# The first two batches of an attention and mixture-of-experts chain rescheduled: a pinned TensorE order, other slots, wider products, low bits on ScalarE

## The chip, the cores and the metric

One core of one Trainium2 chip. The metric is the time of one launch on the device in microseconds (us); each engine (TensorE or PE, VectorE or DVE, ScalarE or ACT, GpSimd or POOL, and SyncE or SP, which issues the transfers) has a queue of its own that it works off in order. A launch is timed three times, and once more with the hardware profiler.

## The reference

Three layers follow each other: Nystrom attention over 8 batches of 576 tokens and 8 heads, a gated feed-forward layer, and a soft mixture of 8 experts. Cut to what matters:

```python
# attention, per batch and head: m = 32 landmarks, the mean over 18 tokens each
A, Bm, C = sm(q, k_lm), sm(q_lm, k_lm), sm(q_lm, k)     # softmax(scale * a @ b.T)
Z = Bm.T / (norms of Bm)
for _ in range(6): Z = 2 * Z - Z @ Bm @ Z
x = A @ Z @ C @ v                                       # [4608, 512] over all batches
# gated feed-forward, d_ff = 1536
g = x @ w_gate; x = (g * sigmoid(g) * (x @ w_val)) @ w_out
# soft mixture of experts, 32 slots
logits = x @ phi
d = softmax over the 4608 tokens; c = softmax over the 32 slots
out = c @ experts(d.T @ x)          # each expert relu(s @ w1) @ w2
```

## The kernel before, in words

The kernel takes the eight batches one after another. x is never written out: for a batch the softmax A (kept as a high part EH and a low part EL of fp32, in the fp32r format) is multiplied by G = (Z C v) w, so that `g_product` (L739) forms for each of 12 chunks of 128 columns of d_ff (`j`) the product of the batch's small block `WB` with the weights `w` into PSUM tiles named g, and evicts them as a high part GH (ScalarE, L765) and a low part GL (VectorE, L779, called `g_low`). `mm3` (L939) then makes the gate (`pg`) and the value (`pv`) of one chunk and one half of 288 tokens with six matmuls each: 24 matmuls a chunk. `unit` (L948) evicts: ScalarE writes u = silu(pg) (L312), VectorE multiplies by pv into hT (L974). Where a pair (chunk, half) stands in `TANH`, silu is made with Tanh on ScalarE (L959) and one more VectorE instruction (L960), since Tanh lies in the same table as Exp, and the table need not be changed.

Around this main stream everything else is interleaved by hand. A chunk has four slots, 0 to 3, one after each group of six matmuls; slot n of a batch is 4 j + i, so a batch has 48. In a slot stand:

- `g_unit(b, j + 1)`, `logits` (eight matmuls of hT with `P_sb`, L794) and `transposes` (VectorE, L799), at the slot numbers of `u` (batches 1 to 7) and `u0` (batch 0);
- the steps of three generators, at the slots listed in `SCHED`: `attention` of the next batch (`at1` to `at3`, 34 steps: landmark sums L333, score products m_a and m_c L541, transposes m_t L631, m_v L653, six Newton products m_n L672, m_w L534), `a_softmax` of the next batch (`am1` to `am3`: maxima, Exp, sums, E), and `softmoe` of the batch before (`sm`, `sm1`: Exp of the logits, the transpose DN L867, the exchange of DN's quarters between partitions by twelve small transfers L879 or, for batch 6, by matmuls m_dr L882, then 144 small matmuls m_d L913 and their sums Sacc L923);
- in batch 0 alone: `conversion` of the float64 weights, twelve of w and twelve of w_out. ScalarE makes the top 32 bits (L176), VectorE shifts (L192) and ORs (L193); with `lw` set for a weight, one ScalarE instruction makes the low bits in place of VectorE's shifts. From w_out, `p_transposes` (m_wt L269), `p_product` (m_p L278) and `p_sum` (m_ps L284) make `P_sb`. The raw weights stream in through a few staging buffers, in the order `loads`; a buffer's next load is issued after its conversion.

Ahead of batch 0 stands its own attention (`first_attention`, until 39 us); behind batch 7 stand the experts and the output. PSUM has three buffers of the tag `x`, which g, m_a, m_c, m_t, m_n, m_v, m_d and the three of batch 0 share. The framework orders each engine's instructions by a planner of its own; `keep_order(PE, middle, ...)` (L1136) ties TensorE's to the order of the program from the mark `middle` on, which is set at batch 1 (L1099).

Of the kernel before, what the change touches and what calls it, by code (L numbers as in the profile page):

```python
# [22 lines left out]
NJ = DFF // 128  # L23
# [31 lines left out]
def nystrom_softmoe_kernel(  # L55
# [681 lines left out]
    def paired(b, j):  # L737
        return 0 < b < nb - 1 and not (b == nb - 2 and j >= NJ - 2)
# [209 lines left out]
    def unit(b, j, slot):  # L948
# [3 lines left out]
        for half in range(2):  # L952
            pg = psp.tile([128, 512], F32, tag="pg", name="pg", bufs=2)
            mm3(pg, b, j, 0, half)
            u = mp.tile([128, HALF], F32, tag="u", name="u", bufs=2)
            by_tanh = 0 < b < nb - 1 and (j, half) in TANH[b > 1]
            if by_tanh:

                act.activation(u, pg[:, 0:HALF], AF.Tanh, scale=0.5)  # L959
                dve.scalar_tensor_tensor(out=u, in0=u, scalar=1.0, in1=pg[:, 0:HALF], op0=ALU.add, op1=ALU.mult)  # L960
            else:
                in_order("silu", u, pg[:, 0:HALF], AF.Silu)
            slot(2 * half)
            pv = psp.tile([128, 512], F32, tag="pv", name="pv", bufs=2)
            mm3(pv, b, j, 1, half)
            o = hT[:, HALF * half:HALF * half + HALF]
            if b == 0 and S_["hp"][2 * j + half]:
                vt = spare[1][:, 128:416]
                act.copy(vt, pv[:, 0:HALF])
                pool.tensor_tensor(out=o, in0=u, in1=vt, op=ALU.mult)  # L970
            elif by_tanh:
                dve.scalar_tensor_tensor(out=o, in0=u, scalar=0.5, in1=pv[:, 0:HALF], op0=ALU.mult, op1=ALU.mult)
            else:
                dve.tensor_tensor(out=o, in0=u, in1=pv[:, 0:HALF], op=ALU.mult)  # L974
            slot(2 * half + 1)
# [5 lines left out]
    TANH = [{(5, 0), (5, 1), (6, 0)}, {(1, 1), (2, 0), (2, 1)}]  # L981
# [105 lines left out]
    for a in range(1, nb):  # L1087
        att, asm = attention(a), a_softmax(a)
        for gen, nm in ((att, "at"), (asm, "am")):
            for r in S_[nm + str(min(a, 3))]:  # L1090
                todo[48 * (a - 1) + r].append(gen)
        sm = softmoe(a - 1)
        for r in S_["sm1" if a == 1 else "sm"]:
            todo[48 * a + r].append(sm)
    prev = None
    n_ins = lambda: len(nc.cur_bb.bb.instructions)
    for b in range(nb):
        if b == 1:
            middle = n_ins()  # L1099
        for j in range(NJ):  # L1100
            p = prev
            def slot(i):
# [27 lines left out]
                if n == (46 if b == 0 else 45) and b + 1 < nb:  # L1130
                    g_unit(b + 1, 0)
                if n == (47 if b == 0 else 46):
# [212 lines left out]
```

## Time and profile before

| | us |
|---|---|
| three timed runs | 676.28, 674.23, 675.02 (median 675.02) |
| profiled execution, its own time | 674.4 |
| its span (first to last instruction) | 672.6 |
| TensorE busy in the span | 623.9 (93%) |
| VectorE busy | 478.0 (71%) |
| ScalarE busy | 298.8 (44%) |
| start to the first product of batch 0 (L748) | 39.2 |
| batch 0 (39.2 to 126.2) | 87.0 |
| batch 1 (126.2 to 201.0) | 74.8 |
| batches 2, 3, 4, 5, each | 65.9 |
| batch 6 | 63.9 |
| batch 7 (528.5 to 589.0) | 60.5 |

A batch ends where VectorE has written its last hT. A time of busy TensorE is from a matmul's start to its modelled end; matmuls overlap, so the distance from start to start tells more than the busy share. The mean granted clock of TensorE over the span is 0.984.

### The profile page before, as it was taken

What the parts mean: (1) busy time and instruction counts of PE and PEld (TensorE: products, weight loads), DVE (VectorE), ACT (ScalarE), POOL (GpSimd) and SP (SyncE); (2) the same over time, 40 slices, a digit from 0 to 9 for tenths busy, and PEclk for the clock granted to TensorE, in tenths of its full rate; (3) what the DMA queues carried; (4) which work ended last, traced back from release to release, by engine and by line L of the source; (5) the groups of instructions that cost most, each with busy time, mean ns of one, the idle gap of its engine ahead of it and who ended that gap; (6) DMA issues with size and microseconds to landing.
All of it is one profiled execution on the core that took longest, in us unless ns stands there. A gap on an engine that the chain in (4) does not pass through costs nothing. (4 is left out here: it accounts for less than half of the span.)

```text
span 672.6 us, 18315 instructions
## 1 busy us (share of the span) xinstructions
PE 623.9 (93%) x7591; PEld 465.8 (69%) x7591; DVE 478.0 (71%) x1154; ACT 298.8 (44%) x764; POOL 73.3 (11%) x81
## 2 busy tenths in 40 slices
PE   5699999998999999999999999999999999989991
PEld 2575667784877877787787778777778777843560
DVE  4999989878578777868785978597856645550441
ACT  2566875445438323732383338233823442320441
POOL 0400012013011101110111012001300000010000
PEclk9799999998999999999999999999999999999996
DMA  8788773233222222222222222122120595699999
GB/s 281 271 322 331 269 280 129 87 113 116 73 72 83 75 72 73 84 75 73 72 86 73 71 87 76 69 71 72 57 86 2 160 378 184 220 288 348 348 369 337
DMA packets 63299, 106.47 MB, mean 158 GB/s; under 512 B 4977, under 2 KB 33009, under 8 KB 61681
## 3 DMA queue, kind: packets, MB, share of 16 engines
q1 hardware_dynamic: 63216, 105.32, 47.1%
q8 instruction: 59, 0.97, 0.6%
q14 instruction: 24, 0.19, 0.1%
HBM read 91.24 MB, written 12.58 MB: 154 GB/s over the span
## 5 line engine op out<-in xcount | busy, mean ns | idle before, releaser
L312 ACT ACTIVATE u<-pg 128x288 f32<-128x288 f32 x174 | 71.9, 413 | 138.4 <-PE pg L945 130.8
L974 DVE TENSOR_TENSOR hT<-u,pv 128x288 f32<-128x288 f32 x174 | 77.7, 447 | 40.1 <-PE pv L945 36.3
L945 PE MATMUL pg<-EH,GH 128*128 128x288 f32 x384 | 93.9, 324 | 2.6 <-ACT GH L765 1.6
L779 DVE TENSOR_TENSOR GL<-g,GH 128x512 fp32r<-128x512 f32 (+1 forms) x122 | 66.4, 572 | 37.7 <-ACT GH L765 37.6
L945 PE MATMUL pg<-EH,GL 128*128 128x288 f32 x384 | 85.7, 299 | 1.7 <-DVE GL L779 1.5
L945 PE MATMUL pv<-EH,GH 128*128 128x288 f32 x384 | 84.0, 298 | 0.0
L945 PE MATMUL pg<-EL,GH 128*128 128x288 f32 x384 | 83.5, 296 | 0.0
L945 PE MATMUL pv<-EL,GH 128*128 128x288 f32 x384 | 82.6, 296 | 0.0
L945 PE MATMUL pv<-EH,GL 128*128 128x288 f32 x384 | 82.2, 295 | 0.0
L765 ACT CAST GH<-g 128x512 fp32r<-128x512 f32 (+1 forms) x122 | 54.2, 495 | 55.0 <-PE g L748 54.9
L945 PEld LDWEIGHTS pg<-EH,GH 128*128 128x128 f32 x384 | 60.0, 189 | 22.8 <-issue 15.5
L799 DVE STREAM_TRANSPOSE HB<-hT 128x576 f32<-128x576 f32 x96 | 74.3, 774 | 1.8
L945 PEld LDWEIGHTS pg<-EH,GL 128*128 128x128 f32 x384 | 62.2, 188 | 4.7 <-DVE GL L779 3.8
L945 PEld LDWEIGHTS pv<-EH,GH 128*128 128x128 f32 x384 | 61.6, 188 | 2.6 <-issue 1.2
L945 PEld LDWEIGHTS pg<-EL,GH 128*128 128x128 f32 x384 | 61.8, 188 | 0.9 <-issue 0.9
L945 PEld LDWEIGHTS pv<-EL,GH 128*128 128x128 f32 x384 | 61.5, 188 | 0.9 <-issue 0.9
L945 PEld LDWEIGHTS pv<-EH,GL 128*128 128x128 f32 x384 | 61.6, 188 | 0.5 <-issue 0.5
L748 PE MATMUL g<-w,WB 64*32 64x512 f32 (+1 forms) x976 | 56.4, 510 | 0.4 <-ACT WB L535 0.4
L794 PE MATMUL l<-hT,P_sb 128*32 128x160 f32 (+1 forms) x768 | 45.2, 298 | 0.8 <-DVE hT L974 0.6
L794 PEld LDWEIGHTS l<-hT,P_sb 128*32 128x32 f32 x768 | 15.2, 108 | 39.8 <-DVE hT L974 16.5
L913 PE MATMUL m_d<-HB,HB 32*32 32x384 f32 x864 | 38.4, 514 | 2.6 <-DMA HB<-DN 2.3
L913 PE MATMUL m_d<-HB,DN 32*32 32x384 f32 x288 | 37.7, 514 | 0.0
(248 smaller groups left out, 946.4 us busy)
## 6 DMA issues: line engine op xcount, KB each, us to landing
k<-in_kT_dram SPq DMA_DIRECT2D x52, 288.0 KB, 3.7
ffn<-in_w_dram SPq DMA_DIRECT2D x13, 1024.0 KB, 9.0
ffn<-in_w_dram SPq DMA_DIRECT2D x24, 512.0 KB, 9.0
HB<-in_w_cat_dram SPq DMA_DIRECT2D x8, 1024.0 KB, 8.0
v<-in_v_dram SPq DMA_DIRECT2D x8, 1024.0 KB, 5.8
q<-in_qT_dram SPq DMA_DIRECT2D x28, 288.0 KB, 3.0
HB<-in_w_out_dram SPq DMA_DIRECT2D x12, 512.0 KB, 5.8
wr<-in_w_cat_dram SPq DMA_DIRECT2D x4, 1024.0 KB, 8.7
```

Source lines behind the costliest of these rows:

```text
L312: i = act.activation(*a, **kw)
L748: pe.matmul(gs[r][32 * hp:32 * hp + 32, 0:256 * n].rearrange("p (u f) -> p u f", u=n), WB[b % 2][64 * r:64 * r + 64, hp, :], w[64 * r:64 * ...
L765: act.copy(H_, g)
L779: dve.tensor_tensor(out=GL, in0=g, in1=GH, op=ALU.subtract)
L794: pe.matmul(L[32 * c:32 * c + 32, 0:32 * k], P_sb[:, j, :], main[:, 0:k, c, :], start=j == 0, stop=j == NJ - 1)
L799: dve.transpose(HB[b % 2][:, S * j:S * j + S].rearrange("p (t r) -> p t r", r=32), hT[:, 0:S].rearrange("p (t r) -> p t r", r=32))
L913: pe.matmul(ms[a][32 * g:32 * g + 32, 0:384].rearrange("p (j f) -> p j f", j=NJ), d_of(a, g, k), hb[32 * a:32 * a + 32, :, 4 * k + g, :], ...
L945: pe.matmul(ps[:, 0:HALF], G_t[b, j, q, sel_][h], e[:, q, ts_], start=n == 0, stop=n == 5)
L974: dve.tensor_tensor(out=o, in0=u, in1=pv[:, 0:HALF], op=ALU.mult)
```

## The change

Nine things, all of them in the order and the place of work; what is computed stays the same.

1. `middle` is set ahead of batch 0, so TensorE's order is the program's there too.
2. `u0` becomes (1, 1, 1): in batch 0 too, `g_unit`, `logits` and `transposes` stand in slot 1.
3. `p` becomes regular: `p_transposes(j)` in slot 4j - 1, `p_product(j)` in 4j + 1, `p_sum(j)` in 4j + 3. All steps of `at1` with matmuls lie in odd slots.
4. `paired` holds in batch 0 from chunk 4 on: one `g_product` of 512 columns for two chunks. The conversions of `w` stand earlier.
5. `lw` is set for weights 2, 3, 5, 7, 9 and 11.
6. In batch 0 three units use Tanh, (4,1), (5,0), (5,1), and `am1` puts its Exp at slots 18, 18, beside those of `at1` at 17, 18.
7. Batch 1: `at2`, `am2`, `sm1` and its three Tanh units are moved some four slots ahead; DN stands at slot 17 (was 20), m_d at 25 (was 24). Its steps now lie nearly all in slot 1 of their chunks.
8. `sm7` for batch 7: DN at slot 10 and the exchange (m_dr) at 13, both 7 before.
9. In a slot that holds steps of several generators, those of `softmoe` now come behind those of `attention` and `a_softmax`, in every batch: m_d behind m_n in slot 25.

The loads of w2, w3, w4 and phi move ahead of v1's, and the load of batch 2's k from slot 44 to 36. At the end of batch 0 `g_unit(1, 0)` and `g_low` stand at slots 45 and 46, as in the other batches.

```diff
@@ -26,27 +26,28 @@
 SEG = S // M
 
 SCHED = {
-    'w': [[-22, 2], [-12, 2], [0, 3], [1, 3], [6, 3], [10, 3], [14, 3], [18, 3], [20, 4], [28, 4], [24, 4], [33, 4]],
-    'o': [[-6, 1], [3, 2], [5, 3], [9, 3], [13, 3], [17, 3], [21, 3], [25, 3], [29, 3], [33, 3], [37, 3], [41, 3]],
-    'p': [[0, 2, 2], [5, 2, 1], [10, 2, 1], [14, 2, 1], [18, 2, 1], [22, 2, 1], [26, 2, 1], [30, 2, 1], [34, 2, 1], [38, 2, 1], [42, 2, 1], [46, 1, 0]],
-    'loads': ['w1', 'q0', 'o0', 'w0', 'v0', 'o1', 'q1', 'v1', 'w2', 'w4', 'p', 'w3'],
-    'at1': [1, 2, 3, 3, 4, 5, 6, 6, 7, 7, 8, 8, 9, 9, 10, 10, 12, 13, 13, 13, 16, 17, 18, 19, 20, 21, 22, 26, 28, 31, 34, 37, 40, 43],
-    'am1': [20, 21, 22, 22, 24, 24, 26, 27, 28, 30, 32, 34, 36, 37, 39, 41, 42],
-    'at2': [-3, -2, -1, 0, 3, 4, 5, 6, 9, 10, 10, 11, 17, 18, 18, 19, 19, 20, 20, 21, 21, 22, 23, 23, 23, 25, 27, 29, 31, 33, 35, 37, 39, 42],
-    'am2': [12, 12, 13, 13, 20, 21, 22, 23, 24, 25, 27, 29, 31, 32, 34, 36, 37],
+    'w': [[-22, 2], [-12, 2], [0, 3], [4, 3], [6, 4], [8, 4], [12, 4], [15, 4], [19, 4], [23, 4], [27, 4], [31, 4]],
+    'o': [[-6, 1], [1, 2], [4, 3], [8, 3], [12, 3], [16, 3], [20, 3], [24, 3], [28, 3], [32, 3], [36, 3], [40, 3]],
+    'p': [[-1, 2, 2], [3, 2, 2], [7, 2, 2], [11, 2, 2], [15, 2, 2], [19, 2, 2], [23, 2, 2], [27, 2, 2], [31, 2, 2], [35, 2, 2], [39, 2, 2], [43, 2, 2]],
+    'loads': ['w1', 'q0', 'o0', 'w0', 'v0', 'o1', 'q1', 'w2', 'w3', 'w4', 'p', 'v1'],
+    'at1': [0, 1, 2, 3, 4, 5, 6, 6, 7, 8, 9, 10, 11, 12, 15, 16, 16, 17, 17, 18, 18, 19, 19, 19, 21, 22, 23, 27, 29, 33, 35, 37, 39, 43],
+    'am1': [11, 12, 13, 13, 18, 18, 20, 22, 23, 24, 25, 28, 30, 31, 32, 33, 36],
+    'at2': [-3, -2, -1, 0, 3, 4, 5, 5, 5, 6, 6, 7, 13, 14, 14, 15, 15, 16, 16, 17, 17, 17, 17, 17, 17, 19, 21, 25, 27, 29, 31, 33, 37, 41],
+    'am2': [7, 8, 8, 9, 16, 17, 18, 19, 19, 20, 22, 23, 25, 26, 27, 28, 30],
     'at3': [-19, -18, -17, -16, -11, -10, -9, -8, -7, -6, -6, -5, 1, 2, 2, 3, 4, 5, 5, 6, 7, 8, 9, 9, 9, 11, 13, 17, 21, 25, 29, 33, 37, 41],
     'am3': [-4, -3, -3, -2, 6, 7, 9, 10, 11, 12, 14, 15, 17, 18, 19, 20, 22],
     'sm': [1, 2, 3, 6, 7, 7, 25, 26, 26, 28],
-    'sm1': [1, 2, 4, 19, 20, 21, 24, 25, 25, 28],
+    'sm1': [1, 2, 4, 15, 17, 18, 25, 26, 26, 28],
+    'sm7': [1, 2, 3, 6, 10, 13, 25, 26, 26, 28],
     'up': [0, 0, 0, 0, 1, 1, 1, 0, 0, 0, 1, 1, 0, 0, 0, 1, 0, 1, 1, 0, 0, 0, 1, 0],
     'hp': [0, 0, 0, 0, 0, 0, 0, 0, 0, 0, 0, 0, 0, 0, 0, 0, 0, 0, 0, 0, 0, 0, 0, 0],
     'lp': [0, 0, 0, 0, 0, 0, 0, 0],
-    'u0': [1, 3, 3, 0],
+    'u0': [1, 1, 1, 0],
     'u': [1, 1, 1, 0],
     'side': {'a': 'Ca', 'b': '', 'c': 'aabCCCbCb', 'd': 'a', '1': 'C', '2': 'baCb', '3': 'baaCba', '4': 'CCb', '5': '', '6': ''},
-    'lw': [0, 0, 0, 0, 0, 0, 0, 0, 0, 0, 0, 0],
+    'lw': [0, 0, 1, 1, 0, 1, 0, 1, 0, 1, 0, 1],
     'lo': [0, 0, 0, 0, 0, 0, 0, 0, 0, 0, 0, 0],
-    'lq': 44,
+    'lq': 36,
     'lv': 26,
 }
 
@@ -735,7 +736,7 @@
     G_t = {}
 
     def paired(b, j):
-        return 0 < b < nb - 1 and not (b == nb - 2 and j >= NJ - 2)
+        return (b > 0 or j >= 4) and b < nb - 1 and not (b == nb - 2 and j >= NJ - 2)
 
     def g_product(b, j, n):
 
@@ -953,7 +954,7 @@
             pg = psp.tile([128, 512], F32, tag="pg", name="pg", bufs=2)
             mm3(pg, b, j, 0, half)
             u = mp.tile([128, HALF], F32, tag="u", name="u", bufs=2)
-            by_tanh = 0 < b < nb - 1 and (j, half) in TANH[b > 1]
+            by_tanh = b < nb - 1 and (j, half) in TANH[min(b, 2)]
             if by_tanh:
 
                 act.activation(u, pg[:, 0:HALF], AF.Tanh, scale=0.5)
@@ -978,7 +979,7 @@
 
     WARM = [3, 4, 3, 2, 2]
 
-    TANH = [{(5, 0), (5, 1), (6, 0)}, {(1, 1), (2, 0), (2, 1)}]
+    TANH = [{(4, 1), (5, 0), (5, 1)}, {(4, 0), (4, 1), (5, 0)}, {(1, 1), (2, 0), (2, 1)}]
     GROUPS = [2, 2, 4, 8, 8, 8, 4]
 
 
@@ -1089,14 +1090,14 @@
         for gen, nm in ((att, "at"), (asm, "am")):
             for r in S_[nm + str(min(a, 3))]:
                 todo[48 * (a - 1) + r].append(gen)
+    for a in range(1, nb):
         sm = softmoe(a - 1)
-        for r in S_["sm1" if a == 1 else "sm"]:
+        for r in S_["sm1" if a == 1 else "sm7" if a == nb - 1 else "sm"]:
             todo[48 * a + r].append(sm)
     prev = None
     n_ins = lambda: len(nc.cur_bb.bb.instructions)
+    middle = n_ins()
     for b in range(nb):
-        if b == 1:
-            middle = n_ins()
         for j in range(NJ):
             p = prev
             def slot(i):
@@ -1127,9 +1128,9 @@
                 if not first:
                     for gen in todo[48 * b + n]:
                         next(gen, None)
-                if n == (46 if b == 0 else 45) and b + 1 < nb:
+                if n == 45 and b + 1 < nb:
                     g_unit(b + 1, 0)
-                if n == (47 if b == 0 else 46):
+                if n == 46:
                     g_low()
 
             prev = (b, j, *unit(b, j, slot))
```

## Rows read from the trace of the kernel before

**Rows 1.** Batches 0, 1, 2: busy PE, PEld, DVE, ACT, POOL; granted clock; DMA.

```profile
39.20:126.20 87.00, 83.24 (x952) 60.89 (x953) 80.23 (x184) 60.39 (x143) 8.75 (x7) 1.00 0.72 262
126.20:201.00 74.80, 71.22 (x864) 53.66 (x864) 55.31 (x131) 31.44 (x82) 10.59 (x10) 0.98 0.27 84
201.00:266.90 65.90, 64.76 (x826) 50.94 (x826) 51.77 (x127) 29.06 (x77) 8.43 (x8) 1.00 0.25 77
```

**Rows 2.** Timeline of TensorE in batch 2: start, us, line, tile, count.

```profile
228.01 1.09 PE L748 MATMUL g<-w,WB 64*32 64x512 f32 x16
229.03 0.47 PE L794 MATMUL l<-hT,P_sb 128*32 128x160 f32 x8
...
229.90 0.52 PE L945 MATMUL pg<-EH,GH 128*128 128x288 f32 x2
...
233.25 0.47 PE L794 MATMUL l<-hT,P_sb 128*32 128x160 f32 x8
```

**Rows 3.** Timeline of TensorE in batch 0: first, one chunk, last.

```profile
40.38 0.40 PE L945 MATMUL pg<-EH,GH 128*128 128x288 f32 x1
...
107.76 0.53 PE L945 MATMUL pv<-EH,GH 128*128 128x288 f32 x2
...
108.75 0.66 PE L748 MATMUL g<-w,WB 64*32 64x256 f32 x16
...
109.59 0.51 PE L945 MATMUL pg<-EH,GH 128*128 128x288 f32 x2
...
110.46 0.58 PE L672 MATMUL m_n<-RV,bd 128*128 128x96 f32 x4
...
125.93 0.53 PE L945 MATMUL pg<-EH,GH 128*128 128x288 f32 x2
```

**Rows 4.** TensorE's waits in batch 0: total us, times, longest; first and last.

```profile
PE pg L945 <- ACT GH L765: 1.6, 2, 0.9
...
PE g L748 <- ACT WB L535: 0.4, 1, 0.4
```

**Rows 5.** Timeline of TensorE in batch 1: m_d starts and goes on.

```profile
157.07 0.83 PE L913 MATMUL m_d<-HB,DN 32*32 32x384 f32 x2
...
161.87 0.51 PE L913 MATMUL m_d<-HB,HB 32*32 32x384 f32 x2 [2.28 <-DMA HB<-DN]
```

**Rows 6.** Busy time by engine and granted clock, inside that m_d.

```profile
162.86:166.27 3.41, 3.41 (x84) 2.41 (x92) 2.86 (x5) 0.00 (x0) 1.49 (x2) 0.50 0.45 138
```

**Rows 7.** Timeline of TensorE in batch 7: m_dr.

```profile
538.53 0.55 PE L882 MATMUL m_dr<-DN,cst 32*128 32x160 f32 x6 [1.92 <-DVE DN L867]
539.48 0.53 PE L882 MATMUL m_dr<-DN,cst 32*128 32x160 f32 x2 [0.40 <-DVE HB L885]
```

**Rows 8.** VectorE by line in batch 0: busy us, mean ns, idle before.

```profile
L192 DVE TENSOR_SCALAR w<-w 128x512 int32<-128x512 int32 x20 | 10.0, 522 | 0.5 <-ACT w L176 0.3
L779 DVE TENSOR_TENSOR GL<-g,GH 128x256 fp32r<-128x256 f32 x24 | 9.2, 416 | 0.5 <-ACT GH L765 0.5
```

**Rows 9.** VectorE by line in batch 1.

```profile
L779 DVE TENSOR_TENSOR GL<-g,GH 128x512 fp32r<-128x512 f32 x13 | 8.6, 686 | 6.2 <-ACT GH L765 6.2
...
L960 DVE SCALAR_TENSOR_TENSOR u<-u,pg 128x288 f32<-128x288 f32 x3 | 1.3, 436 | 0.0
```

**Rows 10.** ScalarE by line in batch 0.

```profile
L176 ACT ACTIVATE w<-HB 128x1024 f32<-128x1024 f32 x6 | 6.9, 1147 | 0.0
...
L312 ACT ACT_TABLE_LOAD x5 | 6.4, 1283 | 0.9 <-DVE stat L608 0.9
```

**Rows 11.** Timeline of VectorE in batch 1: DN.

```profile
152.41 0.34 DVE L867 STREAM_TRANSPOSE DN<-LT 128x160 f32<-128x160 f32 x1
```

**Rows 12.** Timeline of SyncE in batch 1: the exchange of DN.

```profile
152.77 7.81 SPq L879 DMA_DIRECT2D HB<-DN  x12
```

**Rows 13.** Timeline of TensorE in batch 2: m_n behind m_d.

```profile
238.62 0.69 PE L672 MATMUL m_n<-RV,bd 128*128 128x96 f32 x4 [0.66 <-DVE Sacc L923]
```

**Rows 14.** Timeline of VectorE in batch 2: the last reader of m_n.

```profile
240.27 0.28 DVE L688 TENSOR_TENSOR RV<-RV,m_n 128x128 f32<-128x128 f32 x1
```

## The prediction, made before the change was run

> **What bounds the kernel now.** I first cut the span at the batches' last hT and read the table of busy time by stretch. Batches 2 to 5 take 65.9 us each, batch 0 takes 87.0 and batch 1 takes 74.8 [rows 1]: the change works where a batch costs more than the steady one. In batch 2 TensorE is busy in 64.8 of 65.9 us, so TensorE's order is the bound there. In batch 0 TensorE and VectorE are both loaded: 80.2 of 87.0 us on VectorE, 92%, and ScalarE follows with 60.4 [rows 1]. DMA, at a share of 0.72, is no bound yet.
>
> The timeline of TensorE says what a busy TensorE hides. In batch 2 a chunk's 24 main matmuls run in one stretch, 229.90 to 233.25 [rows 2]. In batch 0 the main stream is cut into 46 stretches for 12 chunks (my count; the first begins at 40.38, the one at 125.93 already belongs to batch 1) [rows 3]. The reader should see there that the stretch of six that begins at 107.76 is left for a g product, and the next six at 109.59 for m_n. The view of waits adds five short waits of TensorE in batch 0, 3.9 us in all, the longest 0.9 [rows 4].
>
> In batch 1 one wait stands out: m_d begins at 157.07 and gets going only at 161.87, when the exchange of DN has landed [rows 5]; the granted clock then stands at 0.50 for 3.4 us [rows 6]. In batch 7 m_dr waits 1.92 us for DN [rows 7].
>
> **The sum, part by part.** It is made against the profiled execution's own 674.4 us, which lies 0.6 under the median 675.02 and 1.8 over its span of 672.6.
>
> *Batch 0, departures (changes 1 to 3).* A main matmul costs 0.131 us: 24 and one return take 3.35 us [rows 2], six and one take 0.99 [rows 3], and the difference over 18 gives it. So a break of the stream costs 0.99 - 0.79 = 0.20 us where the array is left for smaller tiles, and 109.59 to 110.46, 0.87 us, makes it 0.08 where the visitor uses the whole array [rows 3]. Of the 46 visits now, 36 have smaller tiles and 10 have none. By the lists in the diff there will be 24: 12 in slot 1, all with small tiles, 12 in slot 3, of which about 6 have some. That is 18 x 0.20 + 4 x 0.08 = 3.9 us. The Trainium skill (TensorEngine Tiling (Array Packing), Key Properties) states that a change of tiling mode drains TensorE, which speaks against half of this regrouping: m_wt and m_ps work in the main stream's own mode, so gathering them would bring nothing. By that rule the term would be 3.6, by one price for every break 4.4; the 0.08 beside 0.20 bears the rule out.
>
> *Batch 0, pairs (4).* Eight products of 0.66 us become four of 1.09 [rows 2, 3]: 5.3 - 4.4 = 0.9 us of TensorE. On VectorE sixteen subtractions of 416 ns become eight of 686 [rows 8, 9]: 1.2 us less.
>
> *Batch 0, low bits and Tanh (5, 6).* Six weights lose two shifts each: 12 x 0.522 = 6.3 us of VectorE [rows 8]. ScalarE gets six instructions over 1024 elements that the trace of before does not show; the nearest row is the top-bits conversion of the same size and the same eight-byte step, 1147 ns [rows 10], and the bounds are its half and its double. That is 6.9 us more (3.4 to 13.8). With the Exps together and Tanh beside them, two of five table loads go, 2.6 us [rows 10]. Three more VectorE instructions of 436 ns cost 1.3 [rows 9]. So VectorE has 80.2 - 6.3 - 1.2 + 1.3 = 74.0 us to do and ScalarE 60.4 + 6.9 - 2.6 = 64.7. ScalarE's addition I cost at nothing: it stays under TensorE and VectorE; without that cover it is a rival below.
>
> *Batch 0 together.* 3.9 + 0.9, and half of the 3.9 us of waits, since most of those are for GH, GL and others behind VectorE's and ScalarE's queues: 6.8 us. Check from VectorE's side: at today's 92%, 74.0 us of work take 80.4, which is 6.6 less. Bounds: 13.0 (VectorE without a gap) and 1.5 (the breaks' 3.9 less 0.1 at each of 24 departures, where the pinned order stands behind a copy).
>
> *Loads, and k of batch 2 earlier.* Nothing: no wait of TensorE in batch 0 names a DMA [rows 4]; bounds 0 and the 0.9 of the longest wait, either way.
>
> *Batch 1 (7).* From DN's start, 152.41, to the last piece of the exchange, 161.87, pass 9.5 us; 7.81 of them are SyncE's issue of twelve transfers [rows 5, 11, 12]. DN and m_d now stand four slots apart, then eight. Eight slots are two chunks of 65.9 / 12 = 5.5 us, 11.0 in all, so the exchange hides with 1.5 us to spare. 4.8 us of waiting go, and 1.7, half of the stretch at half the clock [rows 5, 6]. Five steps leave slots of their own (m_t, m_v, one m_n, m_w, m_d): 5 x 0.20 = 1.0. Against it, 0.6 for change 9 here (next part). Together 6.9, bounds 2.5 (2.7 us of the wait and the clock's 1.7 stay) and 7.5 (nothing for change 9).
>
> *Order in a slot (9), batches 2 to 6.* Now m_n waits 0.66 us behind m_d for a PSUM buffer [rows 13]. Then m_d's third tile waits for m_n's buffer. m_n ran from 238.62 to 239.31, its last reader ended at 240.55 [rows 13, 14], so that wait is up to 1.24 us, and 0.64 without the 0.60 us sum that stood between on VectorE. 0.66 given for 0.64: nothing. Bounds over five batches: 3.3 gained, 2.9 lost.
>
> *Batch 7 (8).* DN gets three slots before m_dr: the 1.92 us go and, as m_dr joins slot 1, 0.20 more. But there g holds two of three PSUM buffers when m_dr wants four: three waits of the 0.40 that one costs now, so 0.8 more [rows 7]. Gain 1.3, bounds 0 and 2.3 (both waits of the rows go).
>
> Sum: 6.8 + 6.9 + 0 + 1.3 = 15.0; 674.4 - 15.0 = 659.4, and at the median 660.0.
>
> **The rivals.** *VectorE was the whole bound in batch 0.* Then the waits inside the stretches go with its load: 74.0 plus some 2 us, a gain of 11 in place of 6.8, 655.8 in all. For it: 92% on VectorE. Against: TensorE has the same share.
>
> *ScalarE comes late.* Top and low bits stand back to back, 2.3 us, in front of a GH eviction of 0.5 to 0.9. Between g and the next chunk lie twelve matmuls, 1.6 us, and slot 3's visit, some 0.8. A conversion that falls there costs 2.3 + 0.9 - 2.4 = 0.8 us of TensorE; six times, 4.8: 664.8. For it: two waits for GH already [rows 4]. Against: with 64.7 of some 80 us ScalarE is still idle a fifth of the time.
>
> *The exchange in batch 1 is late again.* DN needs an Exp, which needs a table load of 1.28 us [rows 10], among four others. If DN slips by 3 us, m_d waits 1.5 and the clock falls: 3.2 with the 1.7 above, 663.2. The Trainium skill (TensorE: Matmul & The Clock Gate, HAM oscillation) says that a DMA wait in a matmul stream is paid again in throttled matmuls; the 0.50 in the trace agrees.
>
> *The pinned order waits (the other side).* In batch 0 the planner now slips ready work in where the program's next is not ready; pinned, each of 24 departures can stand behind an eviction. At 0.63 us each the whole 15.0 are gone; at 0.9, today's longest wait, 24 x 0.9 = 21.6 give 681.6. For it: m_ps stands behind m_p's copy on a ScalarE with more to do. Against: 12 matmuls, 1.6 us, lie between two visits.
>
> *It changes nothing that shows.* Were batch 0 bound by the weights' arrival, its gain would be nil; with the m_d wait still there too, 674.
>
> **How the numbers follow.** Forecast (656.5 to 663) 0.49, VectorE the whole bound 0.15, ScalarE late 0.17, exchange late 0.10, pinned order 0.06, nothing 0.03. The first four are faster by over 0.3%, which is about what a measurement of this kernel can tell from no change: 0.91; same 0.03, slower 0.06. The bounds together reach from 649 to 674; 651 to 668 leaves some two in ten out.
>
> **What would show it.** Batch 0 at about 80 us with 24 stretches of main matmuls, VectorE near 74 us in it, eight L192 shifts of w where there were 20 and three table loads; m_d of batch 1 in under 6 us at a clock of 1.00; batch 1 near 68; m_dr without the wait for DN; batches 2 to 5 unchanged within 0.7. Wrong would make it: waits of TensorE in batch 0 that add up to more than today's 3.9, above all behind GH or m_p's copy, or conversions that wait for a DMA.

## The result, and the profile after

The changed kernel takes 681.94 us (median of 5 runs, 679.85 to 685.37), the kernel before 676.28 beside it (674.23 to 677.8): a ratio of 1.0101, 95% interval 1.0079 to 1.0123. It is slower by 1%, where 2.2% faster was forecast. The profiled execution has a span of 680.2 us, 7.6 more than before. All line numbers from L27 on are one higher than before.

Cut at the last hT of each batch, as in [rows 1], the spans differ so: batch 0 +3.1, batch 1 +0.3, batches 2 to 6 together +2.3, batch 7 -1.3, everything behind it +3.1. Busy time by stretch of the changed kernel, batches 0, 1, 2, 7 and what follows (PE, PEld, DVE, ACT, POOL, granted clock, DMA):

```profile
39.20:129.30 90.10, 77.31 (x892) 60.53 (x891) 76.52 (x171) 62.93 (x141) 8.89 (x7) 0.98 0.63 223
129.30:204.40 75.10, 69.85 (x859) 52.48 (x859) 52.41 (x128) 31.16 (x80) 10.59 (x10) 0.98 0.27 84
204.40:270.70 66.30, 65.67 (x826) 51.12 (x825) 51.27 (x126) 29.39 (x77) 8.30 (x8) 1.00 0.25 77
534.20:593.45 59.25, 58.47 (x708) 45.74 (x706) 33.23 (x75) 22.05 (x57) 0.12 (x1) 1.00 0.78 267
593.45:680.20 86.75, 65.52 (x723) 34.95 (x723) 28.16 (x79) 23.59 (x58) 4.71 (x11) 0.93 0.99 328
```

**Batch 0.** Against [rows 1] TensorE is busy 5.9 us less (83.24 to 77.31), VectorE 3.7 less, ScalarE 2.5 more, and the batch is 3.1 longer all the same. By lines, the changed work is as it was priced (VectorE's shifts of w, ScalarE's low bits and table loads; count, busy, mean ns):

```profile
L193 DVE TENSOR_SCALAR w<-w 128x512 int32<-128x512 int32 x8 | 3.1, 418 | 0.2 <-ACT w L177 0.2
...
L313 ACT ACT_TABLE_LOAD x3 | 3.8, 1283 | 0.1
...
L184 ACT ACTIVATE wr<-wr 128x1024 int32<-128x1024 uint16 x3 | 3.5, 1151 | 0.0
```

What grew is TensorE's waiting, from 3.9 us [rows 4] to 12.6, in seven groups (total, times, longest):

```profile
PE m_wt L270 <- DVE HB L194: 3.5, 1, 3.5
PE m_ps L285 <- ACT HB L280: 3.1, 1, 3.1
PE m_t L637 <- ACT HB L280: 1.9, 1, 1.9
PE m_t L632 <- ACT P_sb L286: 1.6, 1, 1.6
PE m_n L673 <- ACT HB L280: 1.5, 2, 0.8
PE pg L946 <- ACT GH L766: 0.5, 1, 0.5
PE m_a L542 <- ACT HB L280: 0.5, 1, 0.5
```

The second of them can be read on ScalarE's timeline in chunk 0. m_p is done, but its copy (L280) comes at 48.09, behind four conversions of weights that chunks 2 to 4 need; TensorE's m_ps starts only then:

```profile
43.49 1.14 ACT L184 ACTIVATE HB<-HB 128x1024 int32<-128x1024 uint16 x1
44.52 0.62 ACT L766 CAST GH<-g 128x256 fp32r<-128x256 f32 x2
45.03 1.14 ACT L177 ACTIVATE w<-HB 128x1024 f32<-128x1024 f32 x1
46.07 1.13 ACT L184 ACTIVATE HB<-HB 128x1024 int32<-128x1024 uint16 x1
47.07 1.15 ACT L177 ACTIVATE w<-wr 128x1024 f32<-128x1024 f32 x1
48.09 0.28 ACT L280 COPY HB<-m_p 128x128 f32<-128x128 f32 x1
```

```profile
48.42 0.41 PE L285 MATMUL m_ps<-cst,HB 128*128 128x32 f32 x2 [3.07 <-ACT HB L280]
```

The third to fifth and the last are of another kind: m_t, m_n and m_a do not use what m_p and m_ps deliver; they want one of the three PSUM buffers of tag x (e16 below shows it). Behind the wait of 3.5 the granted clock also stands at 0.50, from 57.4 to 60.8; in [rows 1] it is 1.00 throughout.

**Batch 1.** The exchange of DN is in time, but m_d now stands behind m_n in its slot and gets going only when a reader of m_n frees a buffer; the clock is at 0.77 over the stretch:

```profile
167.94 0.69 PE L673 MATMUL m_n<-RV,bd 128*128 128x96 f32 x4
168.56 0.51 PE L914 MATMUL m_d<-HB,DN 32*32 32x384 f32 x1
...
170.13 0.86 PE L914 MATMUL m_d<-HB,HB 32*32 32x384 f32 x3 [0.74 <-ACT RV L680]
```

```profile
168.50:175.80 7.30, 6.56 (x147) 3.30 (x145) 2.26 (x7) 0.79 (x3) 0.00 (x0) 0.77 0.24 75
```

m_d takes 7.2 us with its wait; before it took 10.5, from 157.07 [rows 5] to the next main matmul at 167.56. (In e1, e2, e5, e6, e8 and e10, with the same lists of batch 1, the clock stayed at 1.00 there and m_d took 5.6 to 5.8.) But around it TensorE waits where it did not:

```profile
PE m_t L632 <- ACT CE L313: 1.8, 2, 1.0
PE l L795 <- DVE hT L975: 1.0, 1, 1.0
PE m_d L914 <- ACT RV L680: 0.7, 1, 0.7
PE l L795 <- DVE hT L973: 0.6, 1, 0.6
```

**Batch 7.** m_dr stands in one piece, without the 1.92 and 0.40 of [rows 7]. Its eight matmuls now take 2.03 us to the next main matmul, where they took 1.41 from 538.53 on:

```profile
549.26 2.10 PE L883 MATMUL m_dr<-DN,cst 32*128 32x160 f32 x8
```

**Behind batch 7** nothing was changed, and yet 3.1 us are lost. The chain that ended last (start, us, what) shows 2.18 us inside m_d for which no semaphore, engine or load is named; before, these 48 matmuls ran through in 1.72 (first row). The other 0.9 us were not traced.

```profile
596.15 1.72 PE m_d L913 x48
...
600.60 1.65 PE m_d L914 x41
602.25 2.18 issue
604.43 0.84 PE m_d L914 x7
```

### The profile page after: what moved, and what is told of

Read it like the earlier page. It is cut to its first block, busy times and chain, and to the rows that moved or that the text cites. A ratio compares the mean times of both kernels' runs of the same rounds, so it can differ in the third digit from the quotient of the medians.

```text
span 680.2 us, 18176 instructions
## 1 busy us (share of the span) xinstructions
PE 623.1 (92%) x7527; PEld 466.1 (69%) x7527; DVE 468.8 (69%) x1137; ACT 302.5 (44%) x760; POOL 72.7 (11%) x81
## 5 line engine op out<-in xcount | busy, mean ns | idle before, releaser
L780 DVE TENSOR_TENSOR GL<-g,GH 128x512 fp32r<-128x512 f32 (+1 forms) x114 | 64.7, 598 | 37.7 <-ACT GH L766 37.5
L946 PE MATMUL pv<-EH,GH 128*128 128x288 f32 x384 | 82.1, 295 | 0.0
L800 DVE STREAM_TRANSPOSE HB<-hT 128x576 f32<-128x576 f32 x96 | 74.3, 774 | 1.9
L749 PE MATMUL g<-w,WB 64*32 64x512 f32 (+1 forms) x912 | 54.9, 534 | 0.0
L914 PE MATMUL m_d<-HB,HB 32*32 32x384 f32 x864 | 42.6, 512 | 5.1 <-DVE RV L689 2.2
L914 PE MATMUL m_d<-HB,DN 32*32 32x384 f32 x288 | 41.2, 512 | 0.0
```

Of the source, the lines that this page charges most:

```text
L749: pe.matmul(gs[r][32 * hp:32 * hp + 32, 0:256 * n].rearrange("p (u f) -> p u f", u=n), WB[b % 2][64 * r:64 * r + 64, hp, :], w[64 * r:64 * ...
L780: dve.tensor_tensor(out=GL, in0=g, in1=GH, op=ALU.subtract)
L800: dve.transpose(HB[b % 2][:, S * j:S * j + S].rearrange("p (t r) -> p t r", r=32), hT[:, 0:S].rearrange("p (t r) -> p t r", r=32))
L914: pe.matmul(ms[a][32 * g:32 * g + 32, 0:384].rearrange("p (j f) -> p j f", j=NJ), d_of(a, g, k), hb[32 * a:32 * a + 32, :, 4 * k + g, :], ...
L946: pe.matmul(ps[:, 0:HALF], G_t[b, j, q, sel_][h], e[:, q, ts_], start=n == 0, stop=n == 5)
```

## The experiments

All ran beside the kernel before, whose medians lay between 674.96 and 675.5 us. The stages of a row are those of one profiled execution (that of e11 took 674.26, the slowest of its ten). Batch 0 is given by its end, the last hT of the batch, in us of the span (126.2 before, 129.2 after). Its first main matmul falls between 37.6 and 41.8, which its end does not follow. "Behind" is the time from the last hT of batch 7 to the end.

| run | median us | ratio to before (95%) | batch 0 ends | batch 1 | batch 2 | batch 7 | behind |
|---|---|---|---|---|---|---|---|
| before | 676.28 | | 126.2 | 74.9 | 65.9 | 60.5 | 83.6 |
| after | 681.94 | 1.0101 (1.0079, 1.0123) | 129.2 | 75.2 | 66.3 | 59.3 | 86.7 |
| e1 | 679.85 | 1.0053 (1.0035, 1.0071) | 126.3 | 74.3 | 66.3 | 59.0 | 87.4 |
| e2 | 681.30 | 1.0090 (1.0060, 1.0119) | 127.4 | 73.7 | 66.3 | 60.5 | 87.4 |
| e3 | 679.77 | 1.0071 (1.0048, 1.0094) | 128.7 | 75.2 | 66.3 | 59.0 | 87.0 |
| e4 | 682.32 | 1.0094 (1.0067, 1.0122) | 130.3 | 74.1 | 66.3 | 59.0 | 87.6 |
| e5 | 680.85 | 1.0076 (1.0048, 1.0104) | 128.7 | 73.8 | 66.3 | 60.6 | 87.3 |
| e6 | 681.99 | 1.0095 (1.0060, 1.0129) | 130.8 | 74.0 | 66.3 | 59.0 | 87.0 |
| e7 | 679.80 | 1.0072 (1.0045, 1.0098) | 130.5 | 72.6 | 65.9 | 59.7 | 87.4 |
| e8 | 682.69 | 1.0104 (1.0068, 1.0140) | 130.3 | 74.0 | 66.3 | 59.0 | 87.5 |
| e9 | 683.13 | 1.0109 (1.0082, 1.0137) | 131.8 | 74.8 | 66.3 | 59.0 | 86.1 |
| e10 | 678.68 | 1.0049 (1.0032, 1.0065) | 131.1 | 73.7 | 66.3 | 59.0 | 83.2 |
| e11 | 671.80 | 0.9954 (0.9938, 0.9970) | 127.0 | 73.4 | 65.9 | 60.6 | 83.9 |
| e12 | 671.12 | 0.9932 (0.9911, 0.9953) | 124.6 | 73.8 | 65.9 | 60.6 | 83.7 |
| e13 | 701.90 | 1.0410 (1.0390, 1.0430) | 146.5 | 74.6 | 66.3 | 59.0 | 87.1 |
| e14 | 694.50 | 1.0290 (1.0257, 1.0324) | 140.9 | 74.6 | 66.3 | 59.0 | 87.0 |
| e15 | 680.49 | 1.0072 (1.0045, 1.0100) | 131.8 | 74.0 | 66.0 | 59.0 | 85.6 |
| e16 | 682.17 | 1.0105 (1.0088, 1.0122) | 131.0 | 73.8 | 66.3 | 59.0 | 86.7 |
| e17 | 674.28 | 0.9983 (0.9964, 1.0001) | 127.6 | 72.6 | 65.9 | 60.5 | 84.4 |
| e18 | 678.69 | 1.0044 (1.0022, 1.0066) | 129.8 | 76.0 | 65.9 | 60.5 | 83.6 |

**e1, TensorE's order of batch 0 free again; e18, the kernel before with it pinned.**

```diff
 # e1 against the changed kernel; e18 is the reverse, against the kernel before
-    middle = n_ins()
     for b in range(nb):
+        if b == 1:
+            middle = n_ins()
```

> The changed kernel, with TensorE's order written out from batch 1 on, as before, and not in batch 0. Theory, the pinned order waits: the 12.6 us that TensorE waits in batch 0 are steps that stand at their place in the program behind a copy of ScalarE or VectorE; a planner that may slip ready matmuls in brings the waits back towards the 3.9 of before, and batch 0 falls from 90.1 us to 81 to 85 (8.7 us less waiting, up to 3.9 for breaks that come back); in all 673 to 677. Rival, the engines behind are late: the waits are ScalarE's queue (conversions hoisted in front of copies) or the order of the loads; then batch 0 stays at 88 to 91, the same waits show, and the time at 680 to 682.

> The kernel before with TensorE's order of batch 0 as written, nothing else. Theory, a pinned TensorE waits wherever the written next step is late, however the visits are spread: batch 0 ends 3 to 6 us later (129 to 132), in all 677.5 to 681. Rival, only the crowding of visits into two departures makes the pinned order wait: batch 0 ends within 1.5 us of 126.2, in all 674 to 676.5.

e18 went as its theory said; e1 fell between its two. Freed, batch 0 of the changed kernel ends at 126.3; pinned, with the same lists for batch 0, it ends at 129.2 to 131.1 (after, e4, e6, e7, e8, e10). Pinning alone makes the kernel before 0.44% slower, and its batch 0 ends 3.6 us later. Its waits of TensorE begin with these:

```profile
PE m_p L278 <- DMA HB<-in_phi_dram: 3.0, 1, 3.0
PE m_wt L269 <- ACT P_sb L285: 2.2, 3, 1.2
```

So the order itself costs some 3 us with either set of lists (0.48% between the ratios of the changed kernel and e1, 0.44% in e18). But e1 ends only where the kernel before does: the visits go back to 36 stretches (my count), and one long wait stays:

```profile
PE m_wt L270 <- DVE HB L194: 4.1, 1, 4.1
```

Behind that wait the clock is at half for some 7 us, where [rows 1] has 1.00 all along (59.0 to 66.0 of e1):

```profile
59.00:66.00 7.00, 6.79 (x64) 2.91 (x64) 4.13 (x10) 3.24 (x6) 0.00 (x0) 0.51 0.84 307
```

**e2, loads in the order of before; e3, no low bits on ScalarE; e4, batch 1's lists of before.**

```diff
-    'loads': ['w1', 'q0', 'o0', 'w0', 'v0', 'o1', 'q1', 'w2', 'w3', 'w4', 'p', 'v1'],
+    'loads': ['w1', 'q0', 'o0', 'w0', 'v0', 'o1', 'q1', 'v1', 'w2', 'w4', 'p', 'w3'],
 # e3 instead
-    'lw': [0, 0, 1, 1, 0, 1, 0, 1, 0, 1, 0, 1],
+    'lw': [0, 0, 0, 0, 0, 0, 0, 0, 0, 0, 0, 0],
 # e4 instead: at2, am2, sm1 of before, and
-    TANH = [{(4, 1), (5, 0), (5, 1)}, {(4, 0), (4, 1), (5, 0)}, {(1, 1), (2, 0), (2, 1)}]
+    TANH = [{(4, 1), (5, 0), (5, 1)}, {(5, 0), (5, 1), (6, 0)}, {(1, 1), (2, 0), (2, 1)}]
```

> The changed kernel with the order of the loads as before (v1 ahead of w2, w4, phi, w3). Theory, the pinned order waits whatever comes first: chunk 0 still ends near 50 us, batch 0 at 89 to 91, in all 681 to 683. Rival, the early weights: with w2 to w4 there by 30 us the planner puts their conversions in front of chunk 0's copies on ScalarE; with them later chunk 0 ends at 46 to 47, and batch 0 falls to 85 to 87, in all 677 to 679.

> The changed kernel with the low bits of all weights on VectorE again. Theory, ScalarE late: six instructions of 1.15 us leave ScalarE, the waits behind the copies of m_p and m_t fall by half (5 us), batch 0 to 85 to 87, in all 677 to 679. Rival, the pinned order alone: the waits stay within 1 us; VectorE has 6.3 us more to do (76.5 + 6.3 = 82.8), which at its share of now (0.85) would make 97 us: batch 0 92 to 97, in all 684 to 689.

> The changed kernel with batch 1's three lists and its Tanh units as before (steps spread, eight... four slots between DN and m_d, as it was). Theory, batch 1's gain was eaten by its own new waits (m_t and l behind ScalarE's Exp and VectorE): batch 1 stands at 74 to 76 us with the old stall of m_d back (10 us), in all 681 to 683. Rival, the gain was real and the rest of the change costs it again (order in a slot, work left by batch 0): batch 1 at 78 to 82, in all 685 to 689.

e2: the wait of m_ps falls to 0.4, and m_p waits 3.7 us for phi in its place. Chunk 0 still ends at 50.1. e3: 4.0 us more on VectorE and 5.1 less on ScalarE from 40.4 on take 1.2 off the wait of m_ps and 0.7 off those of m_t and leave the others (m_wt 3.4, m_n 1.5); batch 0 ends at 128.7, 0.5 sooner, and takes 88.1 us from its first main matmul, between the two expectations. Neither engine's load alone set its length. e4: with the stall of m_d back, batch 1 takes 74.1, no more than with the change's lists under change 9.

**e5, ScalarE's order of batch 0 written out too; e9, the products two slots later.**

```diff
             prev = (b, j, *unit(b, j, slot))
+        if b == 0:
+            keep_order(mybir.EngineType.Activation, middle, n_ins())
 # e9 instead
-    'p': [[-1, 2, 2], [3, 2, 2], [7, 2, 2], [11, 2, 2], [15, 2, 2], [19, 2, 2], [23, 2, 2], [27, 2, 2], [31, 2, 2], [35, 2, 2], [39, 2, 2], [43, 2, 2]],
+    'p': [[1, 2, 2], [5, 2, 2], [9, 2, 2], [13, 2, 2], [17, 2, 2], [21, 2, 2], [25, 2, 2], [29, 2, 2], [33, 2, 2], [37, 2, 2], [41, 2, 2], [45, 1, 1]],
-    'u0': [1, 1, 1, 0],
+    'u0': [1, 3, 1, 0],
```

> The changed kernel with ScalarE's order of batch 0 written out too, beside TensorE's. Theory, only TensorE keeps the written order while the planner puts conversions in front of the copies that TensorE's next step waits for: in the changed kernel ScalarE ran five conversions of 1.15 us before m_p's copy (wait 3.1 us), and the top bits of the third w_out piece came 2 us late (wait 3.5 us). With ScalarE in the written order both waits shrink below 1 us each, batch 0 falls from 90.1 us to 83 to 86, in all 676 to 678. Rival, ScalarE simply has too much to do, or the weights arrive too late: batch 0 stays within 1.5 us of 90, in all 680 to 683; a ScalarE that must wait for a weight in the written order may even make it longer.

> The changed kernel with the three visits of each w_out piece (m_wt, m_p, m_ps) two slots later and the logits of batch 0 in slot 3 behind them; order pinned, low bits, pairs and loads as changed. Theory, the visits were put closer together and earlier than ScalarE's and VectorE's chain for a piece can follow, so that TensorE stands at them in either order (pinned or not) and whatever ScalarE does first: two slots, about 3 us, of slack take the waits of m_wt (3.5) and m_ps (3.1) to under 1.5 each, batch 0 falls from 88.6 us (first main matmul to last hT) to 83 to 85.5, in all 677 to 679. Rival, the chain itself is too slow (weights' arrival, 16 KB of w_out per partition through two buffers): the waits move to the later visit, batch 0 stays at 87.5 to 90, in all 680.5 to 683.

Both rivals came true, in e9 with a batch 0 of 91.6 us from its first main matmul, more than its rival said. In e5 the 3.1 us of m_ps are gone, in e9 they are 0.8, but TensorE then waits at the next steps: in e5 1.8 for P_sb's copy, 1.6 behind VectorE's stat and 2.9 for w_out pieces; in e9 m_wt waits five times behind P_sb's copy, 4.1 us. Each remedy moved the waiting and did not end it.

**e13 to e16, m_p and m_ps outside tag x.**

```diff
-        m = psp.tile([128, 512], F32, tag="x", name="m_p", bufs=3)
+        m = now_pv[0][:, HALF:HALF + 128]
...
-        m = psp.tile([128, 512], F32, tag="x", name="m_ps", bufs=3)
+        m = now_pv[0][:, HALF + 128:HALF + 160]
...
+            now_pv[0] = pv
             mm3(pv, b, j, 1, half)
 # e14: e13 with e5's edit. e15: e13's edit on e12. e16: e13 with pg in place of pv
```

> The changed kernel with the results of m_p and m_ps in the free columns of the pv buffer of their slot, not in a buffer of tag x. Theory, two visits per chunk put more products into one departure than the three buffers of tag x hold, so that m_t, m_n and m_a wait for copies of m_p and m_ps (1.9 + 1.6 + 1.5 + 0.5 = 5.5 us) whose data they do not use: these waits go, batch 0 falls from 88.6 us (first main matmul to last hT) to 82.5 to 85, in all 676 to 678.5. Rival, the steps behind those copies were late anyway: the waits return under another name, batch 0 87 to 90, in all 680 to 682.5.

> The same with ScalarE's order of batch 0 written out as well. Theory, what is then left is m_ps behind a copy that conversions overtook (3.1 us) and m_wt behind a late top conversion (3.5): with ScalarE in order most of both goes, batch 0 80 to 83.5, in all 674 to 677. Rival, the w_out pieces and weights are late by themselves: m_wt still waits 2 us and more, batch 0 as in the run with the own columns alone, within 1 us.

> The kernel with the lists of batch 1 and 7, pairs, low bits and Tanh on visits as before, and m_p and m_ps in pv's free columns. Theory, with visits spread as before tag x hardly collides (0.5 us of such waits in the kernel before): batch 0 within 1 us of the same kernel without it (87.0 from the first main matmul), in all 670 to 672. Rival, tag x binds there too: 83 to 85.5, in all 667 to 669.

> The changed kernel with the results of m_p and m_ps in the free columns of the pg buffer of their half chunk. Theory, tag x: the 5.5 us that m_t, m_n and m_a wait for copies of m_p and m_ps go and nothing new comes, batch 0 falls from 88.6 to 90 us (first main matmul to last hT) to 83 to 85.5, in all 676 to 679. Rival, two departures per chunk leave no slack whichever buffers: m_p and m_ps now wait for u, m_wt for its piece, and batch 0 stays at 87.5 to 91, in all 680.5 to 684.

e13 to e15 tell nothing of the cause: in pv's buffer the two products wait for VectorE's reading of pv (the first waits of e13):

```profile
PE pv L285 <- DVE hT L976: 11.7, 9, 4.5
PE pv L279 <- DVE hT L974: 2.6, 1, 2.6
```

e16 is the cleaner one. No wait of m_t or m_n is left, so those were waits for a buffer, as supposed. Batch 0 still ends at 131.0, since the products now wait 7.0 us for u:

```profile
PE m_wt L270 <- DVE HB L194: 3.3, 1, 3.3
PE pg L285 <- ACT u L313: 3.2, 2, 2.9
PE pg L285 <- DVE u L962: 2.1, 2, 1.8
PE pg L279 <- ACT u L313: 1.7, 2, 1.2
```

The theory that tag x makes the loss falls: without those waits the batch is no shorter.

**e6, batch 3's landmark sums held back in batch 1; e7, change 9 undone.**

```diff
-        with tc.issue_after(fence["sum"]) if "sum" in fence else nullcontext():
+        f = fence.get("h" if b == 3 else "sum")
+        with tc.issue_after(f) if f is not None else nullcontext():
...
-        dve.transpose(HB[b % 2]...
+        i = dve.transpose(HB[b % 2]...
+        fence["h"] = getattr(i, "ins", i)
 # e7 instead
-    for a in range(1, nb):
         sm = softmoe(a - 1)
```

> The changed kernel with the eight landmark sums of batch 3 (0.74 us each on VectorE), which the planner puts 5 to 12 slots early into chunks 4 to 6 of batch 1, held back to their slots 29 to 39. Theory, batch 1's gain was eaten by VectorE: it is busy 14.4 of the 14.9 us between 153.6 and 168.5, and l and m_n wait behind it; with 5.9 us less there batch 1 falls from 75.1 us to 71 to 73, in all 678 to 680. Rival, ScalarE's group of Exp (m_t waits 2.1 us for it) or the eight-step crowd itself is the limit: batch 1 stays at 74.5 to 75.5, in all 681 to 682.5.

> The changed kernel with softmoe's steps ahead of attention's in a shared slot, as before. Theory, the order alone costs batches 2 to 5 their 0.4 us each and batch 6 its 0.7: they return to 65.9 and 63.85 us, in all 2.3 less, 679 to 680. Rival, batch 2's other lists or the late landmarks cost it: they stay at 66.3.

e6: both waits of l are gone, and yet batch 1 takes 74.0, as in the runs with the same lists and the landmarks early (73.7 to 74.3 in e1, e2, e5, e8, e10). VectorE's early sums were not the limit. The 74.0 lies between the two expectations, the time in the rival's range. m_t still waits 1.8 us for ScalarE's Exp.

e7: batches 2 to 6 go back to 65.9 and 63.9 exactly, and in batch 1 m_d takes 4.84 us at full clock (batches 1 and 2):

```profile
130.50:203.05 72.55, 67.54 (x860) 51.68 (x859) 52.63 (x128) 30.94 (x80) 10.57 (x10) 1.00 0.27 87
203.05:269.00 65.95, 64.83 (x827) 51.01 (x826) 51.75 (x127) 29.04 (x77) 8.42 (x8) 1.00 0.25 77
```

The order in a slot cost 2.3 us in batches 2 to 6, as the theory said, and 2.6 in batch 1 of the profiled execution. Against e1, e2, e5, e8 and e10, which have the same lists there and a clock of 1.00 in m_d, it cost 1.1 to 1.7; the rest of the 2.6 is the clock of 0.77.

**e8 and e10, small matmuls in the start: the seam of TensorE's code.** They add work that nothing reads.

```diff
     act.activation(warm, one, AF.Exp)
+    m = psp.tile([128, 512], F32, tag="l", name="pad")
+    for _ in range(62):   # e10: range(31)
+        pe.matmul(m[0:32, 0:M], LT[0:64, 0:32], LT[0:64, 32:64], start=True, stop=True)
```

> The changed kernel with 62 tiny matmuls (124 instructions of TensorE) in its start, where TensorE is idle. Theory, the 1.4 to 2.2 us for which TensorE stands in m_d behind batch 7, with nothing to wait for, is the arrival of its next 16 KB of instructions: the pairs of batch 0 took 124 instructions away, so that the seam between two such pieces falls into m_d's fast small matmuls; with 124 put back the seam is where it was, the gap goes, and from the last hT to the end pass 83.5 to 84.5 us in place of 86.7, in all 678 to 680. Rival, the gap comes from the FFN loads or from batch 7's lists: it stays, 86.5 to 87.5, in all 681 to 683.

> The changed kernel with 31 tiny matmuls in its start. The 62 before turned out as 248 instructions of TensorE, one piece of 16 KB almost exactly, so that they left the seam where it was. Theory, code arrival: 31 are 124, half a piece; the seam leaves m_d behind batch 7 as in the kernel before, the gap of 1.7 to 2.2 us goes, and from the last hT to the end pass 83.5 to 84.5 us in place of 86.7 to 87.5, in all 678 to 680. Rival, FFN loads or batch 7's lists: the gap stays, 86.5 to 87.5, in all 681 to 683.

e8 left the gap (1.8 us) where it was, because its arithmetic was wrong. The page of e8 counts 7651 matmuls and as many weight loads, 248 instructions more than the 2 x 7527 of the changed kernel, and one transfer more on the queue of instructions:

```profile
PE 631.8 (93%) x7651; PEld 476.1 (70%) x7651; DVE 468.8 (69%) x1137; ACT 302.7 (44%) x760; POOL 73.1 (11%) x81
...
q8 instruction: 60, 0.98, 0.6%
```

15,054 instructions in 59 transfers are some 255 each; 248 more move the seam by one whole piece, back to its place. e10 has 124 more, as many as the kernel before has within 4 (2 x 7591 against 2 x 7589), and there the gap is gone:

```profile
PE 627.2 (93%) x7589; PEld 472.2 (70%) x7589; DVE 468.6 (69%) x1137; ACT 303.1 (45%) x760; POOL 72.5 (11%) x81
```

```profile
600.83 1.72 PE m_d L914 x48
```

Behind batch 7 pass 83.2 us again. The gap was in every run with the changed kernel's count of instructions or 248 more (1.4 to 2.2 us: after, e1 to e9, e13, e14, e16), and in none with about the count of before (e10, e11, e12, e15, e17, e18; the 85.6 of e15 has another cause, which was not sought). The trace shows the transfer too: of the code queue, q8, one transfer falls into 601.3 to 603.2 of the changed kernel, inside m_d, while none falls into 596.1 to 597.9 before and one into 598.4 to 599.5, behind it.

```profile
q8 instruction: 1, 0.02, 5.8%
```

So the gap is the arrival of the next 16 KB of code in the fast small matmuls of m_d.

**e11, e12 and e17, what can be kept.**

```diff
 # e11 against the kernel before: at2, am2, sm1 and batch 1's TANH of the change, and
+    'sm7': [1, 2, 3, 6, 10, 13, 25, 26, 26, 28],
...
-        for r in S_["sm1" if a == 1 else "sm"]:
+        for r in S_["sm1" if a == 1 else "sm7" if a == nb - 1 else "sm"]:
 # e12: e11, and of batch 0 the change's w, lw, TANH, g_unit at slot 45 and
-        return 0 < b < nb - 1 and not (b == nb - 2 and j >= NJ - 2)
+        return (b > 0 or j >= 4) and b < nb - 1 and not (b == nb - 2 and j >= NJ - 2)
 # with e10's lines. e17: e16 with the edits of e5, e7 and e10
```

> The kernel before with batch 1's lists and Tanh units and batch 7's list of the change, order in a slot and batch 0 as before. Theory, these parts gain when change 9 is left out: batch 1 72.0 to 73.0 us (before 74.85), batch 7 59.0 to 59.7 (60.5), the rest as before, in all 671 to 672.5, faster than before. Rival, batch 1's gain depends on the changed batch 0: batch 1 74 to 76, in all 673.5 to 675.

> As the kernel with batch 1's and batch 7's lists alone, and of batch 0 only the pairs from chunk 4, the low bits on ScalarE and the Tanh units; its visits, loads and their free order as before, and 31 tiny matmuls in the start to keep the seam of TensorE's code. Theory, VectorE and ScalarE did not bound batch 0: 6 us less on VectorE bring the 0.9 us of the pairs and no more, batch 0 ends at 124.5 to 126, in all 670 to 671.5. Rival, VectorE bound it (92% busy): batch 0 ends at 118 to 122, in all 664 to 668.

> The same with ScalarE's order of batch 0 written out, softmoe's steps first in a shared slot, and 31 tiny matmuls in the start. Theory, the causes add up: 2.4 us in batches 2 to 6 and 1 to 2.5 in batch 1 for the order, 3 to 4 behind batch 7 for the seam, batch 0 at 82 to 85: in all 666 to 670. Rival, batch 0 stays at 87 to 90 from its first main matmul: 671 to 675.

e11 and e12 are faster than both kernels, by 0.46% and 0.68% of the kernel before. In e12 VectorE has 4.2 us less to do in batch 0 than in e11 and the batch, from its first main matmul to its end, takes 87.0 us against 85.8 (it begins 3.6 us sooner and ends 2.4 sooner): VectorE did not bound it. e17 joins the edits of e5, e7, e10 and e16 and is not clear of the kernel before (0.9964 to 1.0001); its batch 0 takes 89.1 us from its first main matmul, as the rival said. No run joins e1, e7 and e10; by their ratios they give back 0.48, 0.29 and 0.52% of the 1.01% lost, so together some 673 us, an estimate, if they add.

e11 also shows why batch 7 gains only sometimes (60.6 there). m_dr takes the same 2.03 us, but the main matmuls behind it ran at a clock near its lower level, 1.2 GHz:

```profile
545.00:548.90 3.90, 3.90 (x18) 3.89 (x18) 0.82 (x2) 0.70 (x2) 0.00 (x0) 0.56 1.04 384
```

## Why the prediction was wrong

From 15.0 us less to 7.6 more are 22.6 us: 9.9 in batch 0, 7.2 in batch 1, 2.3 in batches 2 to 6, 3.1 behind batch 7, none in batch 7.

**Batch 0 together: the step that failed is "half of the 3.9 us of waits".** The prices of the work held: 24 stretches of main matmuls (my count), eight shifts, three table loads, 1.15 us for the low bits (1.147 taken), TensorE busy 5.9 us less where the breaks and pairs gave 4.8. But the waits were taken as a remainder that shrinks with the load of VectorE and ScalarE, and they grew to 12.6. They go with the order: pinned, some 3 us are lost under either set of lists (e1, e18). The load of VectorE does not decide (e3, e12). The check "at today's 92%" failed with it, since it took VectorE for the pace. The rival "the pinned order waits" had the right mechanism and the reason against it was wrong: twelve matmuls lie between two visits, but ScalarE can have 4 us of conversions in front of one copy. Its price, 0.9 at each of 24 departures, was wrong in kind: seven groups of waits, two of them over 3 us. That its 681.6 lies 0.3 from the measured 681.94 is luck: it put 21.6 us into batch 0, where 9.9 went, and the rest was lost in batch 1, in the order in a slot and behind batch 7, which it does not know. The bound of 0.1 at each departure was far too narrow, as 12.6 us over 24 departures are 0.5 each.

Batch 0, freed (e1), does not gain what TensorE saved either, and its trace shows where that goes: 4.1 us of waiting for the third w_out piece, and the 7 us at half the clock behind it, some 3.4 lost by half their length, an estimate. Without the two, batch 0 would take some 79 us from its first main matmul, near the 80 that were forecast; no run tests that. The piece was not late from memory: its load was issued at 39.26 and such loads took 9.0 us, but ScalarE made its top bits only at 56.65, behind two conversions of w:

```profile
54.64 1.11 ACT L177 ACTIVATE w<-wr 128x1024 f32<-128x1024 f32 x1
55.65 1.12 ACT L184 ACTIVATE wr<-wr 128x1024 int32<-128x1024 uint16 x1
56.65 1.24 ACT L177 ACTIVATE HB<-HB 128x512 f32<-128x512 f32 x2
```

In the changed kernel the same wait is 3.5. The DMA engines, busy at 0.99 and 0.96 from 50 to 60 us before, are busy at 0.23 and 0.34 there: the loads, moved earlier, ran full and then dry.

```profile
50.00:55.00 5.00, 4.03 (x53) 3.14 (x51) 3.61 (x8) 3.84 (x8) 0.00 (x0) 1.00 0.23 93
55.00:60.00 5.00, 2.48 (x21) 1.26 (x22) 3.54 (x8) 1.50 (x4) 0.00 (x0) 0.74 0.34 93
```

That conversions, by freeing their staging buffers, set the pace of the loads is argued, not shown. The second row shows another price of long waits, which the prediction left out of batch 0: the clock is at 0.74 there. With the same lists e4, e6, e8 and e10 have three stretches of 3.4 us at 0.50 in batch 0, after and e7 have one, each some 1.7 us by half its length, an estimate; from the first main matmul the four take 89.9 to 92.4 us, the two 88.6 and 88.7. The Trainium skill (TensorE: Matmul & The Clock Gate, HAM oscillation) says that a DMA wait is paid again in throttled matmuls; here a wait for a conversion, the 3.5 us of m_wt, was.

**Batch 1: the wait for the exchange went, new waits came.** With change 9 undone m_d took 4.84 us at full clock, under the 6 that were named, and the exchange was hidden: that rival is out. The step that failed is that nothing new would wait: the steps, packed closer together, met 4.4 us of waits (m_t, l, m_n and the two for GL) and 0.7 of m_d behind m_n, where before 2.3 us went to the exchange and 1.3 to others. The other part is the clock, which in this execution fell in m_d again (0.77 over 7.3 us, some 1.7 us). That the stall of m_d had also been time in which VectorE and ScalarE caught up is argued, not shown. With e7's order the lists bring 2.3 us, in e11 1.5, not 6.9.

**Order in a slot: 0 was taken, 2.3 lost in batches 2 to 6.** The term lay inside its bounds (2.9 lost) and on their bad side. The step that failed is the 0.60 taken off the 1.24 for the sum between m_n and its last reader. In the changed kernel no sum stands there, yet that reader ends 1.15 us behind m_n:

```profile
237.04 0.69 PE L673 MATMUL m_n<-RV,bd 128*128 128x96 f32 x4
238.59 0.29 DVE L689 TENSOR_TENSOR RV<-RV,m_n 128x128 f32<-128x128 f32 x1 [0.33 <-ACT RV L688]
```

So the 0.66 that m_n waited for m_d was exchanged for more, and the chunk grew from 9.27 to 9.95 us. In batch 1, where 0.6 was taken, 1.1 to 2.6 were lost.

**Batch 7: right, but not always.** 1.3 was forecast and measured; the waits for buffers, taken at 0.8, made m_dr 0.6 us longer. In five of the runs with its list (e2, e5, e11, e12, e17: 60.5 us) the clock behind m_dr, 0.56 to 0.62 over 3.9 us, took it back; where it was 1.00 (after, e1) the gain stayed. Why it fell in some is open.

**Behind batch 7: no term at all.** Nothing there was edited, and the sum took it as fixed. The pairs took 128 instructions away, and the seam of the code moved into m_d.

The bounds of the sum also leave out one of its parts: with the 0.9 us of the loads either way they reach from 648 to 675, not from 649 to 674. The measured time lies outside of both.

## What to carry to other kernels

A wait of an engine under a full stream is not a remainder of other engines' load. When an order is pinned on one engine, write down for each departure what must be finished on the others and what their queues may put in front, and price the longest such queue, not a mean one, with the matmuls at half the clock that may follow a long wait. When a stall goes and steps move together, ask what each of them will wait for there. And when a change alters the number of instructions, time the untouched stages too: a loss there can be the place of the code, and a few idle instructions in the start tell.

## What had not been expected of the hardware

TensorE's code came in 59 transfers of 16 KB on a queue of its own, one for some 255 instructions. In m_d, where 48 small matmuls and their weight loads take 1.72 us, the engine stood for 1.4 to 2.2 us in 13 of the 20 kernels while the next of these transfers came, shown in the chain of waits only as "issue". Moving the seam by 124 instructions ended it, by 248 did not.

Eight m_dr matmuls of 32 rows, 2.03 us, were followed by main matmuls at a clock of 0.56 to 0.62 in five runs and of 1.00 in the 13 others with the same list, at the same place of the same list: 1.5 us of batch 7 that a single profile would have put down to the change.
